# Moving the second tile pool of an attention and mixture kernel down by 128 bytes in SBUF

## The chip, the cores and the metric

The kernel runs on one core of one Trainium2 chip. The metric is the device time of one execution in microseconds (us). A kernel's time is the median over its runs.

## The reference, cut to what matters

```python
attn = softmax(where(mask, q @ k.T / sqrt(64), -1e9)) @ v     # 4 x 8 heads, 576 positions, head size 64
x = attn as [2304 tokens, 512]
P = exp(x @ w_gate), scaled by rows and columns 8 times       # 2304 x 8
for e in range(8):                                            # first network, w1 512 x 1024, w2 1024 x 512
    out += P[:, e:e+1] * (relu(x @ w1[e]) @ w2[e])
r = relu(out @ w_in); return (r * r) @ w_out                  # second network, 512 x 2048 x 512
```

## The kernel before, in words

**Stages.** The first 112 us or so compute the attention, three matmul groups (scores, transposes, values) to a block, and end with the matmuls of the gate. The rest is 80 *steps*. A step takes 256 of the hidden columns of one expert, or of the second network, through a first layer and a second layer. Steps 0 to 31 run the first network over 1024 tokens of the first pair of token blocks and over 256 single tokens beside them (*pass 1*), steps 32 to 63 run it over the other 1024 tokens (*pass 2*), steps 64 to 71 and 72 to 79 run the second network over the same two parts.

**Products in three matmuls.** Every fp32 operand is split into two fp32r parts, `hi` and `lo`, and a product is `hi*hi + hi*lo + lo*hi`. The first layer (line 479, `product`) has 7 units of 6 matmuls of 512 columns in a step: the moving operand is `x_hi` or `x_lo`, the stationary one a 128x128 block of `blk` or `sum`. The second layer (line 647) has 8 units of 6; the moving operand is `gh` or `gl` and the stationary one a block of `w2` (in the second network the other way round). The single tokens of pass 1 add 24 matmuls of 256 columns in each layer (lines 611 and 676). In the names of the trace, `s<-x_hi,blkh` is the moving operand first and the stationary one second; each matmul has its own weight load (LDWEIGHTS, PEld in the profile), which runs while the matmul before it does.

**Order within a step.** A step issues the first layer of step i and, between its units and after them, the second layer of step i-1. VectorE adds each finished second-layer bank to `acc` (line 659), makes `g`, `gl` and the `lo` parts of the weights (lines 532, 513, 137), and joins two banks of the first layer (lines 580 and 589). In steps 5 to 58 it also narrows int64 words to fp32 (lines 176 to 198). ScalarE makes the `hi` parts, GpSimd four weight sums. The order is written out by hand: each unit is followed by what is due then.

**Two weight sets.** Step i uses `wset[i % 2]`. Set 0 is in the pool `wts`, set 1 is made later, at the head of the pool `post`. So an even step runs its first layer from set 0 and the second layer of the step before, an odd one, from set 1; an odd step runs its first layer from set 1 and the second layer of the even step before it from set 0.

**Where the tiles begin.** Tiles lie one behind the other in each partition. 16,512 bytes are reserved; `pad_x` (384 bytes) puts `ident` at byte 16896 = 33 x 512. `x_hi`, `x_lo`, `xs_hi`, `xs_lo` follow from byte 17408 = 34 x 512, all of them whole multiples of 512 bytes long; `ptile` and `pad_w` fill two multiples more; `raw1`, `sums`, `raw2` and set 0 lie from 83968 = 164 x 512 to 120832 = 236 x 512. Then come `pad_p`, 192 bytes, and the pool `sk`, 448 bytes. The next byte, 121472 = 237 x 512 + 128, is where the attention's tiles begin (`xf`, `mask`, `wg`, then `q`, `k`, `v` and the rest), and, once these are given up, the pool `post`: weight set 1, `acc`, `gh`, `gl`, `s2`, `s3`, `xb`, `sgh`, `sgl`, `g`, `r`, `pp`, `ps`. All of those of `post` are whole multiples of 512 bytes long, so all begin 128 bytes behind a multiple of 512.

Of the kernel before, what the change touches and what calls it, by code (L numbers as in the profile page):

```python
# [9 lines left out]
F32 = mybir.dt.float32  # L10
# [37 lines left out]
def tile_kernel(ctx: ExitStack, tc: tile.TileContext, a):  # L48
# [5 lines left out]
    wts = ctx.enter_context(tc.tile_pool(name="wts", bufs=1))  # L54
# [48 lines left out]
    def new_set(pool, k):  # L103
        wset[k] = {
            n: tuple(pool.tile([128, 1024], F32R, name=f"{n}{h}{k}", bufs=1) for h in ("h", "l"))
            for n in ("blk", "sum", "w2")
        }
# [601 lines left out]
    with tc.manual_schedule():  # L709
# [16 lines left out]
            nc.tensor.matmul(ps[:, :128], warm, warm, start=True, stop=True)  # L726

        new_set(wts, 0)
        wts.tile([128, 48], F32, name="pad_p")
        wr = at.tile([128, 128], F32R, name="wr", bufs=1)  # L730
        xr = at.tile([128, 512], F32R, name="xr", bufs=1)
        nc.vector.tensor_copy(wr, warm)
# [261 lines left out]
```

## Time and profile before

| what | value |
|---|---|
| median of 3 runs | 2019.26 us (2018.82 to 2020.88) |
| profiled execution, its own time | 2018.94 us |
| its span | 2017.2 us |
| TensorE (PE) busy | 1995.1 us, 99% of the span |
| VectorE (DVE) busy | 1544.1 us, 77% |
| ScalarE (ACT) / GpSimd (POOL) busy | 711.5 / 387.5 us |

The span is what the trace covers; the profiled execution's own time is 1.74 us more. Matmuls overlap: the busy time of one matmul (about 393 ns at 512 columns) holds the time that its last columns need to leave the array, while the next one has already begun. What a matmul costs the engine is the distance from its start to the start of the next.

### The profile page before, as it was taken

To read this page: it belongs to the slowest core of one execution; us is meant where nothing else is said; L and a number is where in the kernel's file an instruction comes from. 1 tells how busy PE (TensorE), PEld (TensorE's weight loads), DVE (VectorE), ACT (ScalarE), POOL (GpSimd) and SP (SyncE) were. 2 spreads that over 40 slices of the span, in tenths; PEclk is the share of its full clock that TensorE was granted. 3 is DMA by queue.
4 is the path that set the end of the run, shared out by engine and by line. 5 is a ranking of instruction groups with operands and counts; after the bars stand their busy time and mean duration, and the time that the engine had idled before them with its cause. 6 is when DMAs were issued, how large, how long until landed. Compare 5 with 4: busy or idle time off the path is not lost.

```text
span 2017.2 us, 28458 instructions
## 1 busy us (share of the span) xinstructions
PE 1995.1 (99%) x11584; PEld 1657.7 (82%) x11584; DVE 1544.1 (77%) x2303; ACT 711.5 (35%) x1104; POOL 387.5 (19%) x416
## 2 busy tenths in 40 slices
PE   8999999999999999999999999999999999999999
PEld 6778888888888888888888888888888878887887
DVE  5866677777777777778888888888887786678676
ACT  3443222222332322223433333333333354344442
POOL 4621311111101111112212121121211221123120
PEclk9999999999999999999999999999999999999999
DMA  8512112122222121213322322322221231113111
GB/s 286 178 66 62 61 53 57 61 66 63 66 63 65 48 67 56 62 53 98 117 89 78 100 84 84 89 78 89 84 89 58 82 106 42 43 53 112 55 47 48
DMA packets 71474, 159.33 MB, mean 79 GB/s; under 512 B 6304, under 2 KB 33072, under 8 KB 71344
## 3 DMA queue, kind: packets, MB, share of 16 engines
q1 hardware_dynamic: 71344, 157.52, 24.7%
q8 instruction: 91, 1.49, 0.3%
q14 instruction: 39, 0.32, 0.0%
HBM read 137.49 MB, written 20.00 MB: 78 GB/s over the span
## 4 chain that ended last, share of the span: by engine, by line
PE 94%; DVE 4%; ACT 1%; DMA 1%; issue 0%; SPq 0%; ACTq 0%; DVEq 0%
PE mm L647 43%; PE pt L479 16%; PE s L479 11%; PE xt L479 11%; PE mm L611 6%; PE mm L676 4%; PE xt L351 2%; DVE acc L659 1%; DVE g L532 1%; DVE x_lo L214 1%; PE pt L336 1%; DMA k<-in_k 1%; PE s L299 1%; PE mm L787 1%; DVE suml L137 0%
## 5 line engine op out<-in xcount | busy, mean ns | idle before, releaser
L659 DVE TENSOR_TENSOR acc<-mm,acc 128x512 f32<-128x512 f32 (+1 forms) x630 | 429.0, 683 | 168.1 <-PE mm L647 163.8
L647 PE MATMUL mm<-gh,w2h 128*128 128x512 f32 x1024 | 402.0, 393 | 0.7 <-DVE acc L659 0.7
L647 PE MATMUL mm<-gh,w2l 128*128 128x512 f32 x1024 | 402.0, 393 | 0.0
L647 PE MATMUL mm<-gl,w2h 128*128 128x512 f32 x1024 | 401.4, 392 | 0.0
L538 ACT CAST gh<-g 128x512 fp32r<-128x512 f32 x308 | 191.5, 622 | 592.4 <-DVE g L532 592.3
L146 POOL TENSOR_TENSOR sums<-raw 128x256 f32<-128x256 f32 x80 | 65.9, 823 | 1432.5 <-DVE suml L137 1409.3
L647 PEld LDWEIGHTS mm<-gh,w2h 128*128 128x128 f32 x1024 | 192.2, 188 | 45.0 <-DVE acc L659 1.5
L647 PEld LDWEIGHTS mm<-gl,w2h 128*128 128x128 f32 x1024 | 192.7, 188 | 43.3
L647 PEld LDWEIGHTS mm<-gh,w2l 128*128 128x128 f32 x1024 | 192.2, 188 | 43.1
L513 DVE TENSOR_TENSOR gl<-g,gh 128x512 fp32r<-128x512 f32 x308 | 222.6, 727 | 0.0
L532 DVE SCALAR_TENSOR_TENSOR g<-s,pp 128x512 f32<-128x512 f32 x183 | 128.8, 704 | 96.2 <-PE s L479 94.1
L479 PE MATMUL xt<-x_hi,sumh 128*128 128x512 f32 x320 | 126.4, 395 | 0.0
L479 PE MATMUL pt<-x_hi,sumh 128*128 128x512 f32 x320 | 125.7, 393 | 0.7 <-ACT s L575 0.7
L479 PE MATMUL s<-x_hi,blkh 128*128 128x512 f32 x320 | 126.0, 394 | 0.0
L479 PE MATMUL xt<-x_hi,suml 128*128 128x512 f32 x320 | 125.8, 393 | 0.2
L479 PE MATMUL pt<-x_hi,suml 128*128 128x512 f32 x320 | 125.9, 393 | 0.0
L479 PE MATMUL s<-x_lo,blkh 128*128 128x512 f32 x320 | 125.6, 392 | 0.0
L479 PE MATMUL s<-x_hi,blkl 128*128 128x512 f32 x320 | 125.5, 392 | 0.0
L479 PE MATMUL pt<-x_lo,sumh 128*128 128x512 f32 x320 | 125.5, 392 | 0.0
L479 PE MATMUL xt<-x_lo,sumh 128*128 128x512 f32 x320 | 125.4, 392 | 0.0
L137 DVE TENSOR_TENSOR w2l<-raw,w2h 128x1024 fp32r<-128x1024 f32 x80 | 102.6, 1282 | 12.1 <-ACT w2h L133 12.1
L538 ACT CAST sgh<-g 128x512 fp32r<-128x512 f32 x37 | 23.0, 621 | 224.9 <-DVE g L532 224.9
(158 smaller groups left out, 3980.7 us busy)
## 6 DMA issues: line engine op xcount, KB each, us to landing
raw<-in_w SPq DMA_DIRECT2D x128, 512.0 KB, 3.5
raw<-w SPq DMA_DIRECT2D x32, 512.0 KB, 3.4
v<-in_v SPq DMA_DIRECT2D x24, 384.0 KB, 3.9
pp<-p_dram SPq DMA_DIRECT2D x32, 256.0 KB, 5.7
xb<-in_w_in SPq DMA_DIRECT2D x16, 512.0 KB, 4.7
w<-xb SPq DMA_DIRECT2D x32, 256.0 KB, 2.3
xb<-in_w_out SPq DMA_DIRECT2D x16, 512.0 KB, 4.8
k<-in_k SPq DMA_DIRECT2D x24, 224.0 KB, 4.7
```

The source lines that it names most:

```text
L137: nc.vector.tensor_tensor(out=w[1], in0=src, in1=w[0].bitcast(F32), op=ALU.subtract)
L146: tt(out=c(sums, 0), in0=c(raw1, 2), in1=c(raw1, 3), op=ALU.add)
L214: return lambda: nc.vector.tensor_tensor(out=x_lo[:, k, j], in0=z, in1=x_hi[:, k, j].bitcast(F32), op=ALU.subtract)
L351: nc.tensor.matmul(xt[D * h:D * h + D, pr, c * QB:c * QB + QB], vt[keys, c, head * D:head * D + D], pt[keys, c * 128 + head * QB:c * 128 + ...
L479: nc.tensor.matmul(ps, w[:, c], z[:, x, j], start=start and k == 0, stop=stop and k == 5, skip_group_check=True)
L513: nc.vector.tensor_tensor(out=glo, in0=z, in1=ghi.bitcast(F32), op=ALU.subtract)
L532: nc.vector.scalar_tensor_tensor(out=o, in0=z, scalar=0.0, in1=r, op0=ALU.max, op1=ALU.mult)
L538: after(k + 1, lambda: nc.scalar.copy(ghi, held["g"]))
L611: nc.tensor.matmul(ps[:, n * NSG:n * NSG + NSG], w[:, c], z[:, kc], start=k == 0, stop=k == 3 * KC - 1)
L647: nc.tensor.matmul(ps, lhsT, rhs, start=k == 0, stop=k == 3 * FC - 1)
L659: nc.vector.tensor_tensor(out=dst, in0=ps, in1=dst, op=ALU.add)
L676: nc.tensor.matmul(ps[:, m * NSG:m * NSG + NSG], wt[:, fc, (c + m) * 128:(c + m) * 128 + 128], g[:, fc], start=k == 0, stop=k == 3 * FC - 1,)
```

## The change

The tile `pad_p` shrinks from 48 to 16 fp32 words, that is from 192 to 64 bytes, and everything behind it begins 128 bytes earlier. The attention's tiles and the pool `post` now start at byte 121344 = 237 x 512. Nothing else changes: the same instructions in the same order, the same queues and the same waits.

```diff
         new_set(wts, 0)
-        wts.tile([128, 48], F32, name="pad_p")
+        wts.tile([128, 16], F32, name="pad_p")
         wr = at.tile([128, 128], F32R, name="wr", bufs=1)
```

## Rows read from the trace of the kernel before

**Rows 1.** The page: busy time of PE and DVE.
```profile
PE 1995.1 (99%) x11584; PEld 1657.7 (82%) x11584; DVE 1544.1 (77%) x2303; ACT 711.5 (35%) x1104; POOL 387.5 (19%) x416
```

**Rows 2.** The page: the chain that ended last, by engine.
```profile
PE 94%; DVE 4%; ACT 1%; DMA 1%; issue 0%; SPq 0%; ACTq 0%; DVEq 0%
```

**Rows 3.** Windows of one step, pass 1: even steps 4 to 28; length, busy times.
```profile
265.92:292.17 26.25, 26.25 (x141) 22.68 (x140) 20.16 (x30) 7.69 (x11) 3.31 (x4) 1.00 0.28 81
...
sum 341.18, PE 341.18 PEld 294.77 DVE 260.17 ACT 100.02 POOL 46.52; mean PE 26.24 PEld 22.67 DVE 20.01 ACT 7.69 POOL 3.58
```

**Rows 4.** The same, pass 1: odd steps 5 to 29.
```profile
292.17:318.80 26.63, 26.63 (x141) 22.60 (x139) 18.61 (x27) 7.72 (x11) 3.30 (x4) 1.00 0.19 50
...
sum 346.25, PE 346.25 PEld 293.85 DVE 241.98 ACT 100.23 POOL 43.08; mean PE 26.63 PEld 22.60 DVE 18.61 ACT 7.71 POOL 3.31
```

**Rows 5.** The same, pass 2: even steps 34 to 62.
```profile
1165.08:1185.57 20.49, 20.49 (x92) 16.93 (x90) 18.27 (x27) 6.98 (x10) 3.87 (x4) 1.00 0.33 104
...
sum 307.45, PE 307.45 PEld 253.61 DVE 261.78 ACT 106.90 POOL 50.77; mean PE 20.50 PEld 16.91 DVE 17.45 ACT 7.13 POOL 3.38
```

**Rows 6.** Pass 2: odd steps 33, 37, 41, 45, 49, 53, 57, 59, 61.
```profile
1144.12:1165.08 20.96, 20.96 (x91) 16.89 (x90) 17.73 (x27) 7.08 (x10) 3.35 (x5) 1.00 0.22 68
...
sum 188.70, PE 188.70 PEld 151.98 DVE 157.11 ACT 66.48 POOL 33.28; mean PE 20.97 PEld 16.89 DVE 17.46 ACT 7.39 POOL 3.70
```

**Rows 7.** Pass 2: odd steps 35, 39, 43, 47, 51, 55.
```profile
1185.57:1206.70 21.13, 21.13 (x92) 16.82 (x90) 18.91 (x29) 7.09 (x10) 4.59 (x5) 1.00 0.32 100
...
sum 126.80, PE 126.80 PEld 100.97 DVE 113.46 ACT 42.54 POOL 27.55; mean PE 21.13 PEld 16.83 DVE 18.91 ACT 7.09 POOL 4.59
```

**Rows 8.** The same windows, second network: steps 67, 68, 75, 76.
```profile
1699.44:1725.97 26.53, 26.53 (x128) 22.05 (x127) 17.65 (x25) 10.25 (x16) 3.71 (x4) 1.00 0.14 40
1725.97:1752.06 26.09, 26.09 (x129) 22.06 (x128) 17.66 (x25) 10.25 (x16) 3.71 (x4) 1.00 0.12 41
1897.98:1918.97 20.99, 20.99 (x91) 16.90 (x90) 15.06 (x22) 9.32 (x15) 3.79 (x5) 1.00 0.16 51
1918.97:1939.48 20.51, 20.51 (x91) 16.92 (x90) 14.89 (x22) 9.16 (x15) 3.63 (x5) 1.00 0.15 51
```

**Rows 9.** Timeline of PE in odd step 41: start, own length, line, operands.
```profile
1144.12 0.40 PE L479 MATMUL s<-x_hi,blkh 128*128 128x512 f32 x1
...
1149.71 0.40 PE L647 MATMUL mm<-gh,w2h 128*128 128x512 f32 x1
...
1158.09 0.40 PE L647 MATMUL mm<-gh,w2h 128*128 128x512 f32 x1
```

**Rows 10.** The same in even step 42, and the first matmul of step 43.
```profile
1165.08 0.39 PE L479 MATMUL s<-x_hi,blkh 128*128 128x512 f32 x1
...
1170.54 0.39 PE L647 MATMUL mm<-gh,w2h 128*128 128x512 f32 x1
...
1178.76 0.39 PE L647 MATMUL mm<-gh,w2h 128*128 128x512 f32 x1
...
1185.57 0.40 PE L479 MATMUL s<-x_hi,blkh 128*128 128x512 f32 x1
```

**Rows 11.** Timeline of DVE: line 137 in step 42 and in step 43.
```profile
1170.10 1.21 DVE L137 TENSOR_TENSOR w2l<-raw,w2h 128x1024 fp32r<-128x1024 f32 x1
...
1190.57 1.22 DVE L137 TENSOR_TENSOR w2l<-raw,w2h 128x1024 fp32r<-128x1024 f32 x1
```

**Rows 12.** Timeline of DVE and PE in step 43.
```profile
1192.75 0.69 DVE L659 TENSOR_TENSOR acc<-mm,acc 128x512 f32<-128x512 f32 x1 [0.97 <-PE mm L647]
...
1197.49 0.68 DVE L580 TENSOR_TENSOR s<-xt,s 128x512 f32<-128x512 f32 x1
...
1198.23 0.50 PE L479 MATMUL xt<-x_hi,sumh 128*128 128x512 f32 x1
```

**Rows 13.** Windows: all of step 31, and a stretch in it.
```profile
926.72:964.23 37.51, 36.86 (x195) 31.11 (x193) 33.33 (x45) 16.09 (x26) 13.75 (x11) 1.00 0.29 95
...
931.10:949.22 18.12, 18.12 (x83) 14.55 (x82) 18.09 (x24) 8.15 (x15) 4.66 (x4) 1.00 0.33 103
```

## The prediction

> **What bounds the kernel now.** I read the page first. PE is busy for 99% of the span and DVE for 77% [rows 1], and 94% of the chain that ended last is PE [rows 2]. There is nearly no idle time on PE to win, so the change can only gain by making the matmuls themselves cheaper, and it adds and removes no instruction. The question is whether the place of an operand has a price on PE.
>
> The kernel holds that experiment already: every other step runs from the other weight set, and the sets begin at different remainders of 512. So I cut the trace into windows of one step, from the first first-layer matmul of a step to that of the next. In pass 1 the even steps take 341.18 / 13 = 26.24 us [rows 3], the odd ones 346.25 / 13 = 26.63 [rows 4]. In pass 2 even steps take 307.45 / 15 = 20.50 [rows 5], odd ones 188.70 / 9 = 20.97 [rows 6] or 126.80 / 6 = 21.13 [rows 7]. In the second network it is 26.09 against 26.53 and 20.51 against 20.99 [rows 8]. PE is busy all through these windows, odd and even steps issue the same matmuls, and the granted clock is 1.00 in all of them (2.4 GHz, the upper level), so the odd steps' matmuls are dearer.
>
> Then I put odd step 41 and even step 42 side by side on the timeline of PE. The first 24 matmuls of the first layer take 1149.71 - 1144.12 = 5.59 us in the odd step, 232.9 ns from start to start [rows 9], and 1170.54 - 1165.08 = 5.46 us in the even one, 227.5 ns [rows 10]. The last 30 matmuls of the second layer take 1165.08 - 1158.09 = 6.99 us in the odd step, 233.0 ns each, and 1185.57 - 1178.76 = 6.81 us in the even one, 227.0 ns [rows 9, 10].
>
> Now the places. Even step, first layer: `x` at remainder 0, set 0 at 0. Even step, second layer: `gh` and `gl` at 128, set 1 at 128. Both fast. Odd step, first layer: `x` at 0, set 1 at 128. Odd step, second layer: `gh` at 128, set 0 at 0. Both slow. So what fits is not the remainder itself but whether the moving operand and the weights loaded beside it have the same one: 227 ns when they have, 233 when they differ by 128. The 24 matmuls of the first layer read weight blocks that lie an odd and an even number of 512 bytes apart from `x`, and average 227.5 over both, so 512 is the period that I take.
>
> **The change part by part.** It moves the whole second pool from remainder 128 to 0. `x`, set 0 and the other tiles of the first pools are at 0 already. After it every pair of 512-column matmul operands in the 80 steps has the same remainder, and an odd step should run like an even one.
>
> How many matmuls that is: 42 of the first and 48 of the second layer in an odd step. By the pairs above that is 42 x 5.4 + 48 x 6.0 = 515 ns for a step; the whole steps of pass 2 differ by 20.97 - 20.50 = 0.47 us, since the first matmul of a unit differs less. In pass 1 it is 0.39, so its 48 half-width matmuls give some 0.08 back: they don't gain from equal remainders, they lose a little. I use the differences of whole steps, which hold both.
>
> 1. Pass 1, odd steps 5 to 29 (13): 346.25 - 341.18 = 5.07 us [rows 3, 4].
> 2. Pass 2, nine odd steps: 188.70 - 9 x 20.50 = 4.23 us [rows 5, 6].
> 3. Pass 2, six odd steps at 21.13. They hold 0.16 us more than their neighbours, a wait of PE. DVE had been idle for 0.97 us and then runs without a gap from 1192.75 to the end of line 580 at 1198.17, and the next first-layer unit of PE, at 1198.23, needs the bank that line 580 reads [rows 12]. DVE's work in between doesn't get shorter, while PE's 24 matmuls in it do, by 24 x 5.5 ns = 0.13 us. The wait grows by that. New length: 20.50 + 0.16 + 0.13 = 20.79, so 0.34 saved, and 6 x 0.34 = 2.04 us. Bounds: nothing is saved there (0), or the wait goes as well, 6 x 0.63 = 3.8.
> 4. Second network, odd steps 65, 67, 69: 3 x (26.53 - 26.09) = 1.32; 73, 75, 77, 79: 4 x (20.99 - 20.51) = 1.92 [rows 8].
> 5. Steps 1, 3, 31, 63 and 71 hold changes of pass, new operands or the gate's normalisation. By the rows above they would save 3 x 0.39 + 0.47 + 0.44 = 2.08 together. But step 31 begins at 926.72, and from 931.10 on DVE has no idle time for 18 us (18.09 of 18.12) while PE ends up waiting for it [rows 13]; what PE saves from there on is lost in that wait. Bounds 0 and 2.08; I take 0.9, since step 31 keeps only the start of its saving.
>
> Edits costed at nothing. DVE, ACT and POOL: line 137 reads and writes `w2` of set 0 in step 42, in 1.21 us, and of set 1 in step 43, in 1.22 [rows 11], so 128 bytes have no price there; and DVE's 77% is cover as long as PE sets the pace. The attention's tiles move together, so scores, values and gate keep the distances of their operands; only its transposes, from `ident`, get another distance (288 in place of 416 bytes, or 480 in place of 96). By the price above of some 6 ns a matmul, for under 100 small ones, that is at most 0.6 us either way; I take 0.
>
> **Sum:** 5.07 + 4.23 + 2.04 + 1.32 + 1.92 + 0.9 = 15.5 us. From the profiled execution's own 2018.94 that gives 2003.4. The median of the runs shown, 2019.26, is 0.3 above it, so I forecast 2003.7.
>
> A rule that speaks against all this: the Trainium skill, "SBUF — State Buffer", section "Who interferes with whom", gives PE two independent read ports, one for the moving operand and one for the weight load, and says that "PE and ACT never wait on anyone." By it operand places would have no price and the sum would be 0; this trace disagrees, with 227.0 against 233.0 ns for the same line.
>
> **The rivals.**
>
> *No change.* The pace of odd steps comes from something else that alternates with the step, and not from places. For it: the first layer's banks `s` and `xt` have two buffers, one used in each step, so their bank alternates too. Against it: the second layer goes through three `mm` banks in turn and still shows the split [rows 9, 10]. A milder form is that the period is 1024 and not 512: the pool's new start, 237 x 512, is odd. Against that stands the average over both kinds of weight block. Either way the odd steps stay at 26.63 and 20.97: 2019.3 us. The rule above ends here too. Chance 0.06.
>
> *VectorE takes the place.* With DVE busy for 18.91 us in steps that would last 20.50, its queue could get late for a bank in every odd step of pass 2, not in six. Then items 2 and 3 go: 15.5 - 4.23 - 2.04 = 9.2 saved, 2010.0 us. Against it: even steps with 18.27 us of DVE work already run at 20.49 without such a wait [rows 5]. Chance 0.05, and still faster.
>
> *Slower: one remainder for all is worse.* With all tiles at 0, the operands that DVE and ACT read and write beside the matmuls would start there too, and if that costs a matmul what unequal operands cost now, even steps fall to the odd pace: 16 of 0.39 in pass 1, 16 of 0.47 in pass 2, 8 of about 0.46, some 17.5 us, 2036.8. It decides as soon as even steps take more than 26.24 and 20.50. Against it: in the second layer of even steps `gh`, set 1, `acc`, `g` and `pp` all share remainder 128 and run at 227.0 [rows 10]. Chance 0.03.
>
> **How the numbers follow.** The forecast has 0.86. Its own range: the best case takes all of item 5 (+1.2) and the wait of item 3 (+1.7), 18.4 saved, less 0.4 for the spread of the runs' low end, 2000.3; the worst has neither item 3 nor item 5, 12.6 saved, 2006.7. I give 2000.3 to 2006.9 for the whole, which leaves out the rivals. A difference under 0.2% (4 us) is about what a measurement of this kernel can't tell from none. Faster 0.91 (the forecast and the second rival), same 0.06, slower 0.03.
>
> **What would show it.** Right: in the windows by step, odd and even steps are equal, 26.24 in pass 1 and 20.50 in pass 2; the starts of successive 512-column matmuls lie 227 ns apart in steps of both kinds and both layers; steps 35 to 55 by fours stay longer by 0.2 to 0.3 us. Wrong: odd steps unchanged (places have no price, or the period is longer), even steps slower (the third rival), or waits of PE for DVE in many more steps than the six (the second).

## The result, and the profile after

The changed kernel takes 1995.76 us (median of 4 runs, 1994.5 to 1999.74) against 2019.04 us for the kernel before (4 runs, 2015.45 to 2020.88): a ratio of 0.989, 95% interval 0.987 to 0.991. It is faster, as forecast, but by some 23 us and not by 15.5, and 1995.76 lies below the range of 2000.3 to 2006.9.

The profiled execution took 1999.74 us, its span is 1998.0 us. The page of the changed kernel, busy time and chain by engine, as in [rows 1, 2]:

```profile
PE 1976.1 (99%) x11584; PEld 1660.0 (83%) x11584; DVE 1543.4 (77%) x2303; ACT 711.5 (36%) x1104; POOL 387.8 (19%) x416
...
PE 92%; DVE 6%; ACT 1%; issue 0%; POOL 0%; ACTq 0%; DVEq 0%; POOLq 0%
```

PE is busy for 19 us less with the same 11584 matmuls, and DVE for as long as before: the change acts on PE alone. Still PE sets the pace.

Windows of one step in the changed kernel, grouped as in [rows 3 to 7]: even and odd steps of pass 1 (two lines each), then pass 2: even, nine odd, six odd:

```profile
370.80:396.98 26.18, 26.18 (x140) 22.65 (x139) 20.14 (x30) 7.71 (x11) 3.32 (x4) 1.00 0.25 81
...
sum 340.34, PE 340.34 PEld 294.43 DVE 259.99 ACT 100.25 POOL 46.45; mean PE 26.18 PEld 22.65 DVE 20.00 ACT 7.71 POOL 3.57
...
396.98:423.16 26.18, 26.18 (x140) 22.66 (x139) 18.56 (x27) 7.71 (x11) 3.32 (x4) 1.00 0.16 51
...
sum 340.34, PE 340.34 PEld 294.50 DVE 241.24 ACT 100.21 POOL 43.23; mean PE 26.18 PEld 22.65 DVE 18.56 ACT 7.71 POOL 3.33
...
sum 306.12, PE 306.12 PEld 253.16 DVE 263.32 ACT 107.08 POOL 51.69; mean PE 20.41 PEld 16.88 DVE 17.55 ACT 7.14 POOL 3.45
...
sum 183.81, PE 183.81 PEld 151.95 DVE 156.00 ACT 66.27 POOL 32.83; mean PE 20.42 PEld 16.88 DVE 17.33 ACT 7.36 POOL 3.65
...
1176.72:1197.50 20.78, 20.71 (x91) 16.82 (x90) 18.82 (x29) 7.06 (x10) 4.51 (x5) 1.00 0.31 102
...
sum 124.66, PE 124.25 PEld 100.89 DVE 112.89 ACT 42.35 POOL 27.03; mean PE 20.71 PEld 16.82 DVE 18.81 ACT 7.06 POOL 4.51
```

Odd and even steps are now alike to the hundredth of a microsecond, 26.18 in pass 1. But they are not as long as the even steps were: these fell too, from 341.18 to 340.34 us for thirteen in pass 1 and from 307.45 to 306.12 for fifteen in pass 2. That is the part that the prediction didn't have.

### The profile page after: what moved, and what is told of

Its sections match the earlier page's. It is cut to its first block, busy times and chain, and to the rows that moved or that the text cites. A ratio compares the mean times of both kernels' runs of the same rounds, so it can differ in the third digit from the quotient of the medians.

```text
span 1998.0 us, 28458 instructions
## 1 busy us (share of the span) xinstructions
PE 1976.1 (99%) x11584; PEld 1660.0 (83%) x11584; DVE 1543.4 (77%) x2303; ACT 711.5 (36%) x1104; POOL 387.8 (19%) x416
## 4 chain that ended last, share of the span: by engine, by line
PE 92%; DVE 6%; ACT 1%; issue 0%; POOL 0%; ACTq 0%; DVEq 0%; POOLq 0%
PE mm L647 42%; PE pt L479 15%; PE s L479 11%; PE xt L479 11%; PE mm L611 6%; PE mm L676 4%; PE xt L351 2%; DVE acc L659 1%; PE mm L787 1%; PE s L299 1%; DVE g L532 1%; PE pt L336 1%; DVE gl L513 1%; DVE x_lo L214 1%; DVE blkl L137 1%
```

## The experiments

Each kernel below differs from the changed kernel by the edit shown. Remainders are bytes over a multiple of 512, or of 256 where that is said. The comparison that decides is the length of steps in the trace, and the *80 steps*, from the first matmul of step 0 to the last of the kernel: 1900.18 us before and 1879.95 after. Step windows are given for steps 10, 11 (pass 1) and 41, 42 (pass 2).

**Is it the place itself, or the difference?** All tiles at remainder 128:

```diff
-    const.tile([128, 96], F32, name="pad_x")
+    const.tile([128, 128], F32, name="pad_x")
```

> Everything is moved to remainder 128 of 512: x, both weight sets and the second pool. Theory (only the difference between the moving operand and the weights loaded beside it counts): all pairs are equal, so it runs like the changed kernel, odd and even steps both 26.18 and 20.40 us, time 1994 to 2000. Rival (an operand must itself begin at a multiple of 512): no operand does, every step falls to at least the odd pace of the kernel before, 26.63 and 20.97, time some 2035 to 2040.

Measured: 1998.66 us (1994.58 to 2002.04), ratio to the kernel before 0.9906 [0.9885, 0.9927]. Windows of steps 11 and 41, and of the 80 steps:

```profile
399.16:425.34 26.18, 26.18 (x140) 22.65 (x139) 18.56 (x27) 7.71 (x11) 3.32 (x4) 1.00 0.16 51
1138.16:1158.56 20.40, 20.40 (x92) 16.89 (x91) 17.60 (x27) 7.06 (x10) 3.33 (x4) 1.00 0.22 70
...
115.50:1995.73 1880.23, 1872.94 (x9063) 1578.01 (x9059) 1471.73 (x2156) 664.12 (x983) 328.28 (x348) 1.00 0.22 72
```

No operand begins at a multiple of 512, and every step is as short as in the changed kernel. Beginning at 512 is worth nothing by itself. The rival falls.

**All tiles at remainder 64** asks the same at a place that is no multiple of 128:

```diff
-    const.tile([128, 96], F32, name="pad_x")
+    const.tile([128, 112], F32, name="pad_x")
```

> Everything is moved to remainder 64: x, both weight sets, the second pool. Theory (only the difference counts): as the changed kernel, 26.18 and 20.40, time 1994 to 2000. Rival (a remainder that is no multiple of 128 has its own price): 512-column matmuls some 2 ns dearer as in equal pairs of the run with the second pool at 64, steps of pass 2 about 20.6; the half-width ones of line 676 may fall from 120 to 114 ns, as they did there when sgh and w2 both lay at 64, which takes 0.14 to 0.28 off a step of pass 1.

Measured: 2000.97 us (1994.75 to 2002.7), ratio 0.9912 [0.9892, 0.9933]. The first window reaches from the span's start to step 0; then step 41 and the 80 steps:

```profile
1138.31:1158.71 20.40, 20.40 (x91) 16.89 (x90) 17.59 (x27) 7.06 (x10) 3.33 (x4) 1.00 0.21 70
...
0.00:115.88 115.88, 103.49 (x2526) 82.14 (x2526) 71.22 (x146) 47.02 (x121) 59.30 (x68) 0.91 0.61 206
115.88:1995.97 1880.09, 1873.01 (x9062) 1577.80 (x9059) 1471.57 (x2156) 664.05 (x983) 328.28 (x348) 1.00 0.22 72
```

Again the changed kernel's steps. (The expectation has one thing wrong: the half-width matmuls of 114 ns in the kernel with the second pool at 64 belong to its odd steps, where `sgh` lies at 64 but `w2` of set 0 at 0.) The median is 5 us higher than that of the changed kernel. In the profiled executions the spans are 2000.5 and 1998.0 us, and of these 2.5 us 115.88 - 113.52 = 2.36 lie before step 0, where the granted clock averaged 0.91; this stretch comes up again below.

**How far apart is unequal?** Five values for the second pool, with `x` and set 0 at 0:

```diff
-        wts.tile([128, 16], F32, name="pad_p")
+        wts.tile([128, N], F32, name="pad_p")   # N = 24, 32, 64, 80, 112 puts it at 32, 64, 192, 256, 384
```

> The second pool begins at remainder 32, x and set 0 at 0. Theory with one price for any unequal pair: the 80 steps at 1898 to 1901 us. If the price falls with the distance: 1888 to 1895. If 32 bytes are too little to count: 1880, as the changed kernel.

> The second pool begins at remainder 64; x and set 0 stay at 0. Theory with one price for any unequal pair: odd steps 26.63 and 20.97, time 2015 to 2021. Price by distance: half of it, odd steps about 26.40 and 20.70, time about 2007. If only multiples of 128 matter less than that, for instance any multiple of 64 being free: 26.18 and 20.40, 1994 to 2000.

> The second pool begins at remainder 192 (64 below the next multiple of 256), x and set 0 at 0. Theory with a period of 256: a price as at 64, the 80 steps at 1898 to 1901 us. If only the distance upwards counts, more than at 128: over 1903.

> The second pool begins at remainder 256, x and weight set 0 stay at 0. Theory with one price for any unequal pair: odd steps as in the kernel before, 26.63 and 20.97, time 2015 to 2021. If the price grows with the distance: odd steps over 27.0 and 21.4, time about 2036. If the period is 256 and not 512: odd steps 26.18 and 20.40, time 1994 to 2000.

> The second pool begins at remainder 384, which is 128 below the next multiple of 512; x and set 0 stay at 0. Theory with one price, and also a price by distance taken around the period: as the kernel before, odd steps 26.63 and 20.97, time 2015 to 2021. A price that grows with the remainder itself: odd steps over 27.4 and 21.9, time about 2055.

The window of the 80 steps in the kernel before, and in these five in the order 32, 64, 192, 256, 384:

```profile
112.46:2012.64 1900.18, 1894.65 (x9062) 1578.87 (x9059) 1471.96 (x2156) 664.69 (x983) 328.44 (x348) 1.00 0.23 71
```

```profile
108.29:2012.28 1903.99, 1898.46 (x9062) 1576.01 (x9059) 1471.65 (x2156) 665.13 (x983) 328.78 (x348) 1.00 0.21 71
```

```profile
111.12:2010.23 1899.11, 1893.43 (x9062) 1574.29 (x9059) 1471.63 (x2156) 666.12 (x983) 328.50 (x348) 1.00 0.22 71
```

```profile
108.64:2003.28 1894.64, 1888.69 (x9062) 1573.25 (x9059) 1472.03 (x2156) 664.45 (x983) 328.90 (x348) 1.00 0.22 71
```

```profile
112.79:1993.06 1880.27, 1873.12 (x9062) 1578.04 (x9059) 1471.86 (x2156) 665.69 (x983) 328.52 (x348) 1.00 0.22 72
```

```profile
114.43:2014.66 1900.23, 1894.76 (x9062) 1578.76 (x9059) 1471.89 (x2156) 665.82 (x983) 328.74 (x348) 1.00 0.22 71
```

Times: 64: 2015.81 us, ratio 0.9992 [0.9982, 1.0002]; 256: 1996.61 us, 0.9894 [0.9874, 0.9914]; 384: 2017.06 us, 1.0003 [0.9989, 1.0017]; 32 and 192 in one run each, 2018.59 and 2009.59 us. A difference of 256 bytes is free: the period is 256 and not the 512 that I took, and 384, which is 128 over 256, costs what 128 cost. Every other difference costs, 32 bytes as much as 128 and more (24 us over the changed kernel), 64 some 19 and 192 some 15. So the price doesn't grow with the distance. As a sum over the 80 steps one price for all fails too: 192 missed its expectation by 3 us and 32 by as much on the other side.

But the 80 steps mix two widths of matmul. Pass 2 (steps 32 to 63) has 512-column matmuls alone; its window in the changed kernel, in the kernel before, and at 32, 64 and 192:

```profile
958.10:1615.26 657.16, 655.91 (x2883) 539.58 (x2881) 568.03 (x814) 234.14 (x336) 124.10 (x132) 1.00 0.26 88
...
964.23:1629.89 665.66, 664.97 (x2883) 540.22 (x2882) 568.15 (x814) 234.42 (x336) 124.17 (x132) 1.00 0.27 86
...
961.05:1628.64 667.59, 666.91 (x2882) 539.71 (x2881) 567.89 (x814) 234.66 (x336) 124.13 (x132) 1.00 0.26 86
...
960.75:1626.62 665.87, 665.14 (x2883) 539.72 (x2881) 567.98 (x814) 234.91 (x336) 123.99 (x132) 1.00 0.26 86
...
956.75:1622.87 666.12, 665.41 (x2882) 539.82 (x2881) 567.98 (x814) 234.22 (x336) 124.19 (x132) 1.00 0.26 86
```

There 64, 128 and 192 cost nearly the same, 8.7, 8.5 and 9.0 us, and 32 costs 10.4. What sets 64 and 192 apart in the 80 steps lies in the other stages, mostly in pass 1 with its half-width matmuls. At 64 bytes the direction counts as well. In step 41 the first 24 matmuls of the first layer and the last 30 of the second are 233.3 and 229.4 ns apart in the kernel with the second pool at 64, and 229.9 and 233.3 in the one with it at 192: the full price where the weights lie 64 bytes above the moving operand modulo 256, and under half of it where they lie 64 below. At 128 both layers pay it in full, 233.0 and 233.2. Why is not shown.

**Which operands?** Set 1 alone at 0, and all behind it at 128:

```diff
         new_set(post[0], 1)
+        post[0].tile([128, 32], F32, name="pad_s", bufs=1)
```

> Weight set 1 begins at remainder 0, but acc, gh, gl and the rest of the second pool stay at 128. Theory (moving operand against the weights beside it): the first layer is fast in both kinds of step (x 0, both sets 0) and the second layer slow in both (gh 128 against sets at 0), so odd and even steps become alike at 48 x 6 ns over the changed kernel, about 26.47 in pass 1 and 20.69 in pass 2; even steps get slower than in the kernel before (26.25, 20.50). Time 2015 to 2022. Rival (only where the weights begin counts): all weights are at 0, so 26.18 and 20.40, time 1994 to 2000.

Measured: 2019.25 us (2018.18 to 2027.03), ratio 1.0014 [1.0002, 1.0027]. Steps 10, 11, 41, 42:

```profile
372.73:399.21 26.48, 26.48 (x141) 22.61 (x139) 20.15 (x30) 7.71 (x11) 3.32 (x4) 1.00 0.27 80
399.21:425.69 26.48, 26.48 (x141) 22.61 (x139) 18.62 (x27) 7.71 (x11) 3.32 (x4) 1.00 0.16 50
1146.86:1167.61 20.75, 20.75 (x92) 16.89 (x91) 17.61 (x27) 7.07 (x10) 3.37 (x5) 1.00 0.20 68
1167.61:1188.35 20.74, 20.74 (x91) 16.89 (x90) 18.41 (x27) 7.01 (x10) 3.89 (x5) 1.00 0.31 102
```

Odd steps got faster than before the change and even ones slower, so that both are alike, as the theory said. With all the weights at multiples of 512 the gain is gone: what counts is the moving operand together with the weights. The price is 0.30 us a step in pass 1 and 0.35 in pass 2.

**The other engines' tiles.** In this kernel `s2`, `s3`, `xb`, `sgh`, `sgl`, `g`, `r`, `pp` and `ps` are back at 128:

```diff
+            if i == 0:
+                post[0].tile([128, 32], F32, name="pad_s", bufs=1)
             for n in ("s2", "s3"):
```

> Weight set 1, acc, gh and gl at remainder 0 as in the changed kernel; s2, s3, xb, sgh, sgl, g, r, pp and ps, which VectorE, ScalarE and GpSimd work on, back at 128 (sgh and sgl feed the half-width matmuls of the single tokens too). Theory: only the matmul operands count, 512-column matmuls stay at 227 ns and steps of pass 2 at 20.40; pass 1 between 26.10 and 26.20 since the half-width ones don't gain from equal remainders. Time 1993 to 2000. Rival (places of the other engines' tiles disturb PE): steps of both kinds and passes over 20.5 and 26.3, time over 2005.

Measured: 1997.57 us (1996.4 to 1999.08), ratio 0.9902 [0.9887, 0.9916]. Steps 11 and 41:

```profile
393.79:419.97 26.18, 26.18 (x141) 22.65 (x140) 18.56 (x27) 7.72 (x11) 3.32 (x4) 1.00 0.19 51
1132.80:1153.20 20.40, 20.40 (x91) 16.89 (x90) 17.59 (x27) 7.07 (x10) 3.33 (x4) 1.00 0.21 70
```

Nothing changes. Whether these tiles lie at 0 or at 128 doesn't matter to PE, and the gain of the change doesn't come from them.

**The attention.** Its tiles go back to their old bytes:

```diff
+    xfp.tile([128, 32], F32, name="pad_a")
     xf = xfp.tile([128, KC, NTOK], F32, name="xf")
```

> The attention's tiles go back to where they were before, the second pool stays at the changed place. Theory: the gain lies in the 80 steps alone; from the first matmul of step 0 to the last 1880 us as in the changed kernel, time 1994 to 2000, the start of step 0 anywhere between 111 and 115.5 as in the runs so far. Rival (part of the gain is the attention's): 2 to 3 us slower than the changed kernel, above 1998.

Measured: 1998.0 us (1994.55 to 2004.12), ratio 0.9913 [0.9892, 0.9935]. The stretch before step 0, and the 80 steps:

```profile
0.00:108.18 108.18, 95.96 (x2525) 76.06 (x2525) 71.22 (x146) 47.02 (x121) 59.23 (x68) 0.98 0.65 220
108.18:1988.28 1880.10, 1873.00 (x9063) 1577.99 (x9059) 1471.51 (x2156) 664.05 (x983) 328.20 (x348) 1.00 0.22 72
```

The 80 steps keep the whole gain. Whether the attention itself gains or loses by its place is not shown; the median doesn't tell, since the stretch before step 0 varies by itself: it took 108.18 us here with a granted clock of 0.98, 113.52 in the changed kernel's profile with 0.92, and 115.88 with 0.91 in the run with all at 64 (108.29 with 1.00 in the one with the second pool at 32), while the 80 steps always had 1.00. In that stretch PE isn't busy throughout (95.96 of 108.18 us here), and its clock is at the lower level for part of it, more in one execution than in another.

**Which weights: a matmul's own, or the next one's?** A kernel in which a matmul and its own weights are equal everywhere, and only at a change of layer the moving operand is 128 bytes off the weights that are being loaded for the next matmul:

```diff
-        wset[k] = {
-            n: tuple(pool.tile([128, 1024], F32R, name=f"{n}{h}{k}", bufs=1) for h in ("h", "l"))
-            for n in ("blk", "sum", "w2")
-        }
+        t = lambda n: tuple(pool.tile([128, 1024], F32R, name=f"{n}{h}{k}", bufs=1) for h in "hl")
+        wset[k] = {n: t(n) for n in ("blk", "sum")}
+        pool.tile([128, 32], F32, name=f"pad_s{k}", bufs=1)
+        wset[k]["w2"] = t("w2")
...
-    const.tile([128, 96], F32, name="pad_x")
+    const.tile([128, 56], F32, name="pad_x")
...
-        wts.tile([128, 16], F32, name="pad_p")
+        wts.tile([128, 112], F32, name="pad_p")
```

> x and the first-layer weights of both sets lie at one remainder, w2 of both sets, gh and gl 128 bytes further, so a matmul and its own weights are equal everywhere, and only where one layer follows the other (8 times in a step of pass 2) does a moving operand meet the next matmul's weights 128 bytes off. Theory (what counts is the weight load that runs beside the matmul, that of the next one): every step runs at the even pace of the kernel before, 26.25 and 20.50 us, 5 to 7 us more than the changed kernel over the 80 steps. Rival (a matmul's own weights count): 26.18 and 20.40, as the changed kernel.

Measured: 2005.32 us (2000.99 to 2007.06), ratio 0.9929 [0.9906, 0.9951]. Steps 10, 11, 41, 42, and the 80 steps:

```profile
371.20:397.45 26.25, 26.25 (x141) 22.68 (x140) 20.15 (x30) 7.70 (x11) 3.33 (x4) 1.00 0.28 81
397.45:423.69 26.24, 26.24 (x140) 22.67 (x139) 18.57 (x27) 7.70 (x11) 3.33 (x4) 1.00 0.15 51
1138.33:1158.81 20.48, 20.48 (x92) 16.93 (x90) 17.58 (x27) 7.06 (x10) 3.33 (x4) 1.00 0.22 70
1158.81:1179.29 20.48, 20.48 (x92) 16.93 (x90) 18.42 (x28) 6.99 (x10) 3.90 (x4) 1.00 0.31 104
...
113.24:1998.67 1885.43, 1878.63 (x9062) 1580.30 (x9059) 1471.48 (x2156) 664.34 (x983) 328.96 (x348) 1.00 0.22 72
```

Every step now has the length that only the even ones had before the change [rows 3, 5], and the 80 steps cost 5.48 us more than in the changed kernel, within the 5 to 7 expected. The weight load that counts is the one that runs beside the matmul, that of its successor. And this is what the even steps lost before.

The trace of the kernel before shows it matmul by matmul. In even step 42, at a change from the first layer to the second:

```profile
1170.08 0.39 PE L479 MATMUL pt<-x_lo,sumh 128*128 128x512 f32 x1
...
1170.31 0.40 PE L479 MATMUL pt<-x_hi,suml 128*128 128x512 f32 x1
1170.31 0.19 PEld L647 LDWEIGHTS mm<-gh,w2h 128*128 128x128 f32 x1
```

The last matmul of a unit runs beside the load of the other layer's weights. By the starts in whole nanoseconds it takes 233 ns at each of the seven changes within the step, and the first matmul behind it 230; apart from the three at the head of the step all others take 226 or 227. It isn't the change of the moving operand by itself either: with set 1 alone at 0, the last first-layer matmul ahead of each change in step 41 takes 226 or 227, though `gh` comes next and lies 128 bytes off `x`; there the next weights don't.

**The half-width matmuls.** With the second pool at 64 the matmuls of line 611 had sped up in odd steps, so `xs_hi` and `xs_lo` alone went to remainder 192 (the weights 64 bytes further, modulo 256), first in one run and then with more; in a last kernel `sgh` and `sgl` too:

```diff
+    big.tile([128, 48], F32, name="pad_h")
     xs_hi = big.tile([128, KC, NSG], F32R, name="xs_hi")
...
-    big.tile([128, 112], F32, name="pad_w")
+    big.tile([128, 64], F32, name="pad_w")
...
+            if i == 0:                                      # the last kernel only
+                post[0].tile([128, 48], F32, name="pad_s", bufs=1)
             for n in ("s2", "s3"):
```

> The changed kernel with xs_hi and xs_lo alone moved to remainder 192, so that the weights of the half-width first-layer matmuls lie 64 bytes further than their moving operand, modulo 256. In the run with the second pool at 64 such matmuls started 117 ns apart and not 120. If that holds by itself: 24 x 3 ns = 0.07 us less in a step of pass 1 and of steps 64 to 71, the 80 steps at 1877 us. If it came there from the unequal matmuls before them: 1880 or a little more, as the changed kernel.

> The kernel of the run with xs_hi and xs_lo at 192 once more, for a time with an interval: steps as there (26.03 in pass 1, 25.95 in steps 66 to 70), the 80 steps at 1874.7 us, and a time 5 us below the changed kernel, 1989 to 1995. If its one time was chance: 1994 to 2000.

> sgh and sgl moved to remainder 192 as well, so that w2 lies 64 bytes further than the moving operand of the half-width second-layer matmuls too. If 64 bytes by itself speeds half-width matmuls up: another 24 x 6 ns = 0.15 us off each step of pass 1 (25.88), the 80 steps near 1870.5 us, time 1985 to 1991. If it depends on what ran before them: pass 1 at 26.03 or slower, the 80 steps at 1874.7 to 1876.

Measured: 1994.05 us in the one run; 1991.13 us (1990.02 to 1994.29), ratio 0.9881 [0.9865, 0.9898] with more runs; 1992.2 us (1990.11 to 1994.05), ratio 0.9881 [0.9866, 0.9896], with `sg` moved too. The 24 half-width matmuls of the first layer in step 11, first start and the start of what follows, in the changed kernel and with `xs` at 192:

```profile
420.28 0.28 PE L611 MATMUL mm<-xs_hi,blkh 128*128 128x256 f32 x1
...
423.16 0.40 PE L479 MATMUL s<-x_hi,blkh 128*128 128x512 f32 x1
```

```profile
414.19 0.29 PE L612 MATMUL mm<-xs_hi,blkh 128*128 128x256 f32 x1
...
416.93 0.39 PE L480 MATMUL s<-x_hi,blkh 128*128 128x512 f32 x1
```

2.88 / 24 = 120.0 ns each against 2.74 / 24 = 114.2. Step 11 of the two kernels with `xs` at 192, alone and with `sg`, and the 80 steps:

```profile
390.90:416.93 26.03, 26.03 (x140) 22.51 (x139) 18.56 (x27) 7.69 (x11) 3.32 (x4) 1.00 0.21 51
...
108.86:1983.74 1874.88, 1867.81 (x9062) 1573.30 (x9059) 1471.61 (x2156) 663.70 (x983) 328.26 (x348) 1.00 0.22 72
```

```profile
393.75:419.80 26.05, 26.05 (x141) 22.55 (x139) 18.54 (x27) 7.67 (x11) 3.32 (x4) 1.00 0.15 51
...
111.57:1987.00 1875.43, 1868.20 (x9063) 1574.00 (x9059) 1471.50 (x2156) 662.99 (x983) 328.88 (x348) 1.00 0.22 72
```

`xs` at 192 takes 5.07 us off the 80 steps (1879.95 to 1874.88), where 3 were expected from a pace of 117 ns, and makes the shortest 80 steps of this study. The times by themselves don't tell it from the changed kernel: the intervals of the ratios overlap, 0.9865 to 0.9898 and 0.987 to 0.991. Moving `sg` alike gains nothing more: the half-width matmuls of both layers then start some 118 ns apart, where they had been at 120 in the second layer and at 114 in the first. So a difference of 64 bytes has no fixed price for them. That what runs before them has a part in it fits this, and is not shown.

## Why the prediction was wrong

The mechanism held, and the size was off. The trace of the 80 steps gained 1900.18 - 1879.95 = 20.23 us where the sum said 15.5.

**The step that failed** is the sentence that after the change "an odd step should run like an even one", with the even step of before as the measure. It took the even steps as free of unequal pairs. Within a unit they were, but a step changes layer 8 times in pass 2, the change into it counted, and there an `x` at 0 ran beside the load of a `w2` block of set 1 at 128, or a `gh` at 128 beside set 0's `blk`. The rows for it stood ahead of the prediction and weren't used: between the two stretches that I divided, the 36 matmuls of alternating units in step 42 take 1178.76 - 1170.54 = 8.22 us [rows 10], 228.3 ns each and not 227.0. That is 0.05 us more than 36 x 227.0, and about what the prediction lacked between its 515 ns a step by pairs and its 0.47 us by whole steps; it put this down to the first matmul of a unit. The same step in the changed kernel's timeline:

```profile
1161.76 0.39 PE L647 MATMUL mm<-gh,w2h 128*128 128x512 f32 x1
...
1169.92 0.39 PE L647 MATMUL mm<-gh,w2h 128*128 128x512 f32 x1
...
1176.72 0.39 PE L479 MATMUL s<-x_hi,blkh 128*128 128x512 f32 x1
```

8.16 / 36 = 226.7 ns, the same as the last 30, 6.80 / 30 = 226.7. The kernel with unequal pairs at these changes alone puts 5.48 us on this term, which covers the 4.7 that the sum lacked.

By items, as the sum put them, with what the two traces give:

| item | predicted | measured |
|---|---|---|
| 1. pass 1, 13 odd steps | 5.07 | 346.25 - 340.34 = 5.91 |
| 2. pass 2, nine odd steps | 4.23 | 188.70 - 183.81 = 4.89 |
| 3. pass 2, six odd steps | 2.04 | 126.80 - 124.66 = 2.14 |
| 4. second network, 7 odd steps | 3.24 | 3.74 |
| 5. steps 1, 3, 31, 63, 71 | 0.9 | 0.62 |
| even steps, 40 | 0 | 2.95 |

Items 4 and 5 and the last row are differences of step lengths, cut as in [rows 3 to 8].

**Item 3** was right in its mechanism too, and its number is partly luck. The wait for DVE grew; timeline of DVE and PE in step 43 after the change, as in [rows 12]:

```profile
1183.72 0.69 DVE L659 TENSOR_TENSOR acc<-mm,acc 128x512 f32<-128x512 f32 x1 [0.90 <-PE mm L647]
...
1188.46 0.68 DVE L580 TENSOR_TENSOR s<-xt,s 128x512 f32<-128x512 f32 x1
```

```profile
1189.19 0.50 PE L479 MATMUL xt<-x_hi,sumh 128*128 128x512 f32 x1
```

From the start of line 659 to that of line 580 DVE takes 4.74 us, as before (1197.49 - 1192.75), and PE starts its unit 0.73 us after line 580 begins, where it was 0.74. These steps are 20.78 long against 20.79 forecast, but as 20.40 + 0.38 and not as 20.50 + 0.29: the neighbours fell further than forecast and the wait grew by more, and the two cancel.

**Item 5**: step 31 saved nothing (37.51 before, 37.52 after), as it would if DVE's unbroken work there [rows 13] took all of it; no run tests that.

**The rest** of the miss is the distance of the medians, 23.3 us, from the 20.2 that the traces show. The stretch before step 0 took from 108.2 to 115.9 us in the profiles of this study, with kernels of either kind at both ends, and the four times of the changed kernel lie 5.2 us apart. The kernel before moved as well: beside the experiments its medians were 2016.11 us (19 runs), 2017.35 (13), 2020.28 (7) and 2015.92 (7). My low end allowed 0.4 us for all that. But 20.2 us from 2019.26 would have been 1999.0, below the range by itself. That these 3 us are the clock's is argued from the rows of the two kernels above and not shown for the timed runs themselves.

**The rivals.** *No change* is out: places do have a price, and the rule of the Trainium skill, "SBUF — State Buffer", section "Who interferes with whom", that the prediction set against the trace fails in each of the runs with unequal pairs (233 against 227 ns in the kernel before). The milder form of this rival, a period of 1024, is out too; the period is shorter than I took and not longer. *VectorE takes the place*: the waits stayed in the six steps, but for 0.21 us more in step 33 than in its neighbours. *Slower, one remainder for all*: even steps got faster, and the run with the other engines' tiles at 128 shows no influence of their places.

## What to carry to other kernels

Compare the distance from one matmul's start to the next between stretches that should be alike, by buffer, not the busy time of a matmul; here it was 227 against 233 ns and told of 20 us. For matmuls of 512 columns like these, give the moving operand and the weights loaded beside it (those of the next matmul) equal places modulo 256 bytes. A pad of a few words does it, and the tiles of the other engines needed none here. When a faster half is taken as the measure of the other, look whether it is free of the same cost itself, above all where one kind of work follows another.

## What the runs showed of the hardware that was not expected

- The period is 256 bytes: a second pool 256 bytes off runs the 80 steps in 1880.27 us, 128 or 384 off in 1900.2.
- For 512-column matmuls differences of 64, 128 and 192 bytes cost nearly the same in sum (8.7, 8.5 and 9.0 us in pass 2), and 32 costs more (10.4); at 64 it is 6.6 ns a matmul one way round and about 3 the other.
- What is paid at a change of layer is paid by the last matmul ahead of it, beside which the next weights load (233 ns and not 227), and in part by the first one behind it (230).
- Half-width matmuls go by other rules: 120 ns with equal places; 114 with the weights of the first layer alone 64 bytes further than the moving operand; 118 in both layers when both lie so.
- The granted clock of PE before step 0 averaged between 0.91 and 1.00 in the executions shown, of nearly the same program, and that stretch took 115.88 us at the one and 108.29 at the other.
